# First batch of an mLSTM + Fourier-mix kernel: head outputs with tokens on the partitions instead of transposed afterwards

## The chip, the core and the metric

One core of a Trainium2 chip runs the whole program. The metric is device time in microseconds (us) of one execution, given as the median of several executions; lower is better. Engines are named as in the profile: PE is TensorE (PEld its weight loads), DVE is VectorE, ACT is ScalarE, POOL is GpSimd, SP is the engine that issues the transfers.

## The reference, cut to what matters

Two blocks follow each other. The first is an mLSTM cell with B = 4 batches, H = 8 heads, S = 768 tokens and head dimension D = 40:

```python
for t in range(S):
    m_new = np.maximum(f_gate[:, :, t] + m, i_gate[:, :, t])
    f_stab = np.exp(f_gate[:, :, t] + m - m_new)
    i_stab = np.exp(i_gate[:, :, t] - m_new)
    ...
    C = f_stab * C + i_stab * outer(vt, kt)
    n = f_stab * n + i_stab * kt
    h_tilde = C @ qt
    denom = np.maximum(np.abs(n . qt), 1.0)
    y[:, :, t] = sigmoid(o_gate) * h_tilde / denom
```

Its output, heads side by side, is x with 4 x 768 x 320 numbers. The second block takes the real part of a Fourier transform of x over tokens and over features, adds it to x (u), normalises each row of u, and computes u + relu(un @ w_ch1) @ w_ch2 with a hidden width of 1280. All in float32.

## The kernel before

The recurrence is worked in chunks of L = 128 tokens, NT = 6 chunks for a batch. In a chunk, the output of each head is the sum of two products: one with the state carried in from the chunks before (C and n side by side, 41 columns a head, since the values have a column of ones attached), and one inside the chunk (scores of queries and keys, weighted by a matrix W of exponentials, times the values). Then each head's 40 columns are divided by its 41st and multiplied by the output gate.

The edits are in the first batch (b = 0), whose chunks run by `plan_mlstm`. The order of all work is written by hand: `at(slot, phase, function, ...)` files a step under a time slot and a phase, and `run` issues the steps in that order. Each engine works off its own instructions strictly in the order of issue, so a step filed earlier goes ahead on its engine's queue. For chunk c the slots start at s = 3c. The steps that matter, with their lines:

- `mlstm_scores` (L609): scores ps, 8 heads, with tiles of 64 x 64 of the array.
- `mlstm_exp` (L563): ACT makes W from the PSUM bank pM that PE filled (`spread_max`, L235).
- `mlstm_scale_q` (L571): the queries times their decay, qg. For c = 1 and 2 from PSUM by DVE (L576), later by POOL (L580) after a one-element copy (L579) that reads the finished gate of chunk c-2, so POOL waits for it.
- `mlstm_scale_v` (L582), `mlstm_decay` (L602): POOL prepares values and state.
- `mlstm_weigh` (L618): DVE multiplies scores into W (L622).
- `mlstm_from_state` (L624) and `mlstm_from_chunk` (L633): the two products, added up in the PSUM tile hb (`first_heads_ps`). The state and the values are the weights (64 columns: the 41 of one head, then the first of the next), and the 128 tokens move. So hb holds features on the partitions and tokens along the columns, two heads in a column block.
- `mlstm_to_state` (L639), `mlstm_add` (L658): the next state, pc on PE and the addition on DVE (L661, L663).
- `mlstm_heads` (L647): ACT copies hb, 128 x 512, to SBUF (hT, L650). `mlstm_turn` (L652): PE transposes it in four blocks into the PSUM bank px (L656).
- `mlstm_finish` (L767): DVE takes the 41st columns (den: L785, L786, L787), makes gate over denominator (so, L789), and multiplies (x, L776). The gate's tanh is ACT's (`mlstm_tanh`, L665).
- `mlstm_rows` (L797): in chunks 1 and 4 one row of x has its place in another chunk; three small copies move it (L801 ACT, L803 DVE, L805 ACT).

All products go through `product` (L598), so the profile lists them at L599; the tile names tell them apart. A float32 product shows as two matmul records.

After the chunks come the folds of x for the Fourier transform (`mix_fold`, L895, DVE and POOL), its products (`mix_products`, L975; `mix_feat`, L995), u with its statistics (`mix_add`, L1018), transposes to put (L1065), and the first hidden products (L1163). Pieces of the weights w_ch1, which arrive as 64-bit floats, are put together by DVE in between (`Piece`, L477 to L499). Some products without use (`idle_products`, L143, tile pi) stand on PE ahead of the fold products: each of two products of 256 columns is issued in pieces of 85 or 86 columns, and every piece loads the same 128 x 128 weights. The other three batches use `plan_halves`, which already holds tokens on the partitions and is not touched.

Of the kernel before, what the change touches and what calls it, by code (L numbers as in the profile page):

```python
# [10 lines left out]
FP = mybir.dt.float32  # L11
# [7 lines left out]
B, H, S, D = 4, 8, 768, 40  # L19
L = 128  # L20
NT = S // L
NP = H // 2
LH = L // 2
NS = S // LH
D1 = D + 1
# [5 lines left out]
TG = NT // 2  # L31
# [8 lines left out]
NK = HALF + 2  # L40
# [17 lines left out]
def kernel(  # L58
# [15 lines left out]
    nc = tc.nc  # L74
# [19 lines left out]
    def bank(name, shape, n=None):  # L94

        return ps_m.tile(shape, FP, name=name, tag=f"pm{next(turn) if n is None else n}")


    ident = const.tile([L, L], FP, name="ident")
# [20 lines left out]
    hT_bufs = []  # L120
# [7 lines left out]
    def at(slot, phase, fn, *args):  # L128
        plan.setdefault((slot, phase), []).append((fn, args))
# [10 lines left out]
    def columns_of(n, parts):  # L140
        return [slice(i * n // parts, (i + 1) * n // parts) for i in range(parts)]
# [8 lines left out]
    def gates(gp):  # L150
# [7 lines left out]
        shift = gp.tile([BH, NT, L], FP, name="shift")  # L158
        m_in = gp.tile([BH, NT, 1], FP, name="m_in")
        F = gp.tile([BH, NT, L], FP, name="F")  # L160
        hT_bufs.extend(gp.tile([L, 4, L], FP, name=f"h{n}") for n in range(2))
        M, Mq = (gp.tile([L, NT, L], FP, name=name) for name in ("M", "Mq"))
        g, wk = (x_bufs[1].rearrange("p c m -> p (c m)")[0:n, i * S:(i + 1) * S].rearrange("p (c t) -> p c t", t=L)
                 for i, n in enumerate((L, BH)))
# [355 lines left out]
    chunks = {}  # L520
# [77 lines left out]
    def product(out, w, x, start):  # L598
        nc.tensor.matmul(out, w, x, start=start, stop=True, skip_group_check=True)  # L599
# [24 lines left out]
    def mlstm_from_state(b, c):  # L624

        k = chunks[b, c]
        k.ph = first_heads_ps[:, :, 0:2 * L].rearrange("p hip (m t) -> p hip m t", t=L)
        for p in range(0, NP, 2) if c > 0 else ():
            for hip, i in TILES:
                r, n = slice(hip * 64, hip * 64 + D), (p + i) * D1  # L630
                product(k.ph[half(i), hip, p // 2, :], k.C[0][r, n:n + LH], k.qg[r, p + i, :], p == 0)

    def mlstm_from_chunk(b, c):  # L633
        k = chunks[b, c]
        for h in range(H):
            hip, p = h // NP, h % NP
            product(k.ph[half(p % 2), hip, p // 2, :], k.v[:, h * D1:h * D1 + LH], k.W[:, h, :], c == 0 and p < 2)

    def mlstm_to_state(b, c):  # L639
        k = chunks[b, c]  # L640
# [6 lines left out]
    def mlstm_heads(b, c):  # L647
        k = chunks[b, c]
        k.hT = hT_bufs[c % 2]
        nc.scalar.copy(out=k.hT.rearrange("p (hip m) t -> p hip m t", hip=2), in_=k.ph)  # L650

    def mlstm_turn(b, c):  # L652
        k = chunks[b, c]
        k.px = bank("px", [L, 4, L], 1)
        for n in range(4):
            nc.tensor.transpose(k.px[:, n, :], k.hT[:, n, :], ident)  # L656

    def mlstm_add(b, c):  # L658
        k = chunks[b, c]
# [20 lines left out]
    def half(n):  # L680
        return slice(n * LH, (n + 1) * LH)
# [85 lines left out]
    def mlstm_finish(b, c, part=None):  # L767

        k = chunks[b, c] if part in (0, -1) else chunks.pop((b, c))
        if c == 0:  # L770
            xs[b] = x_bufs[b % 2]
            nc.gpsimd.memset(xs[b][:, :, DM:DM + 1], 0.0)
        h1 = k.px.rearrange("p (a n) (i e) -> p a (n i) e", a=2, i=2) if b == 0 else k.ph
        def tokens(rows, to):
            x, sc = (t.rearrange("p (a h d) -> p a h d", a=2, d=D) for t in (xs[b][rows, to, 0:DM], k.so[rows]))
            nc.vector.tensor_tensor(out=x, in0=h1[rows, :, :, 0:D], in1=sc, op=OP.mult)  # L776

        if part == 1:
            return tokens(slice(0, L), c)
        den = tp.tile([L, H], FP, name="den", tag="den")  # L780

        def two(t):
            return t.rearrange("p (a h) -> p a h", a=2)

        nc.vector.tensor_scalar(out=two(den), in0=h1[:, :, :, D], scalar1=-2.0, scalar2=2.0, op0=OP.mult, op1=OP.max)  # L785
        nc.vector.scalar_tensor_tensor(out=two(den), in0=h1[:, :, :, D], scalar=2.0, in1=two(den), op0=OP.mult, op1=OP.max)  # L786
        nc.vector.reciprocal(out=den, in_=den)  # L787
        sc = k.so.rearrange("p (h d) -> p h d", d=D)
        nc.vector.scalar_tensor_tensor(out=sc, in0=sc, scalar=1.0, in1=den.unsqueeze(2).to_broadcast([L, H, D]),  # L789
                                       op0=OP.add, op1=OP.mult)  # L790
        if b == 0:
            scaled[c] = k.so
        if part != -1:
            tokens(*((slice(0, 1), c - 1) if part == 0 else (slice(0, L), c)))


    def mlstm_rows(b, c, part):  # L797

        spare, x = s_last[0:1, 0:DM], xs[b][0:1, :, 0:DM]
        if part == 0:  # L800
            nc.scalar.copy(out=spare, in_=x[:, c - 1])  # L801
        elif part == 1:
            nc.vector.tensor_copy(out=x[:, c - 1], in_=x[:, c])  # L803
        else:
            nc.scalar.copy(out=x[:, c], in_=spare)  # L805

    def plan_mlstm(b):
        for c in range(NT):
            s, end = 3 * c, c == NT - 1
            if c > 0:  # L810
                at(s, FILL, mlstm_exp, b, c, 0)
                at(s + 1, FILL - 0.5, mlstm_exp, b, c, NP)
                at(s, FILL_PE + (3.5 if end else 2), mlstm_scores, b, c)
            at(s, FILL, mlstm_scale_v, b, c)
            at(s if c == 2 else s + 1, FILL + 0.1, mlstm_scale_q, b, c)
            at(*((6, FILL + 0.25) if c == 1 else (s + 2, FILL)), mlstm_decay, b, c)
            at(s + 1, FILL + (0.2 if end else -0.4), mlstm_weigh, b, c)
            at(s + 2 if end else s + 3, FILL_PE, mlstm_from_state, b, c)
            at(s + 2 if end else s + 3, FILL_PE + (2 if end else 3), mlstm_from_chunk, b, c)
            if not end:  # L820
                at(s + 3, FILL_PE + 3, mlstm_to_state, b, c)
                at(s + 4, FILL - 0.3, mlstm_add, b, c)
            at(*((17, FILL_PE + 2.6) if end else (s + 4, FILL - 0.27)), mlstm_heads, b, c)
            at(*((16, FILL + 0.02) if end else (s + 4, FILL - 0.25)), mlstm_tanh, b, c)
            t, phase = ((5, 2.5), (8, 2.5), (11, 2.5), (14, 2.5), (16, 0.5), (17, 2.8))[c]
            at(t, FILL_PE + phase, mlstm_turn, b, c)
            t, phase = ((6, 0.3), (9, -0.3), (12, -0.3), (15, -0.3), (16.5, 0.4), (18.5, 0))[c]
            if c == 4:
                at(t, FILL + phase, mlstm_finish, b, c, 0)
                at(17, FILL + 0.09, mlstm_finish, b, c, 1)  # L830
            else:
                at(t, FILL + phase, mlstm_finish, b, c)
        for c, part, t, phase in ((1, 0, 7, 0.3), (1, 1, 9, -0.2), (1, 2, 10, -0.1), (4, 0, 16, 0.01),
                                  (4, 2, 18, 0)):
            at(t, FILL + phase, mlstm_rows, b, c, part)

# [138 lines left out]
    def mix_products(p, out, i, m):  # L975
        fm = slice(i * PAD + m.start, i * PAD + m.stop)
        kw = dict(stop=(p == 0), skip_group_check=True)
        if i == 0 and p == TG - 2:
            nc.tensor.matmul(out[:, 0:NK:2], fe[:, p, fm], ds_sb[:, p, 0, 0:NK:2], start=False, **kw)
            nc.tensor.matmul(out[:, 1:NK:2], fe_odd[:, m], ds_sb[:, p, 0, 1:NK:2], start=False, **kw)  # L980
        else:
            nc.tensor.matmul(out, fe[:, p, fm], ds_sb[:, p, i], start=(p == TG - 1), **kw)

    def mix_seq_out(b, i):
        k = mixes[b]
# [9 lines left out]
    def mix_feat(b, p, part=slice(None)):  # L995

        k = mixes[b]  # L1000
        m = slice(COL[p], COL[p] + L)
        if part.start in (None, 0):
            k.pu[p] = bank("pu", [L, DM + 1 + NC], MIX[b - 1]["u"][p] if b > 0 else None)
        pu = k.pu[p]
        if b == 0:
            products = ((pu[:, 0:DM + 1], k.Z[:, 0, m], dd_sb[:, 0]), (pu[:, 0:DM + 1], k.Z[:, 1, m], dd_sb[:, 1]),
                        (pu[:, 0:DM + 1], k.Zt[:, m], dd_sb[:, 2]))
        else:
            products = ((pu[:, 0:NC], k.Z[:, 0, m], dd_sb[:, 0, 0:NC]), (pu[:, NC:DM], k.Z[:, 1, m], dd_sb[:, 1, 1:HALF_D]),
                        (pu[:, 0:DM], k.Zt[:, m], dd_sb[:, 3, 0:DM]))  # L1010
        if p == TG - 2:
            own = first_heads_ps[:, 1, 0:NC] if b == 0 else pu[:, DM + 1:]
            z, zt = (t[:, LAST:LAST + 1].to_broadcast([L, L]) for t in (k.Z[:, 0], k.Zt))
            products += ((own, z, dd_sb[:, 0, 0:NC]), (own, zt, dd_sb[:, 3, 0:NC]))
        for i, (o, z, t) in list(enumerate(products))[part]:
            nc.tensor.matmul(o, z, t, start=(i == 0 or b == 0 and i == 3), stop=(i in (2, 4)), skip_group_check=True)  # L1016

    def mix_add(b, c):  # L1018

# [662 lines left out]
```

## Time and profile before

| What | us |
|---|---|
| median of 3 runs | 379.64 |
| lowest and highest of them | 377.9, 385.28 |
| the profiled execution | 378.71 |
| its span, first to last instruction | 376.9 |

| Engine | busy, us | share of the span |
|---|---|---|
| PE | 370.8 | 98% |
| PEld | 275.6 | 73% |
| DVE | 283.0 | 75% |
| ACT | 171.5 | 46% |
| POOL | 133.2 | 35% |

The granted TensorE clock is 1.0 throughout. A timeline line reads: start, length, engine, source line, operation, tile written <- tiles read, the tile of the array as rows*columns for PE, the size of what moves, and the count of instructions merged into the line. Brackets hold the idle time of that engine before it and what ended that. The end of a matmul is modelled, so spacing is read from start to start. The batch-0 chunks take from about 11 to 40 us of the span, the fold products and feature products from 40 to 55.5.

### The profile page before, as it was taken

To read this page: it belongs to the slowest core of one execution; us is meant where nothing else is said; L and a number is where in the kernel's file an instruction comes from. 1 tells how busy PE (TensorE), PEld (TensorE's weight loads), DVE (VectorE), ACT (ScalarE), POOL (GpSimd) and SP (SyncE) were. 2 spreads that over 40 slices of the span, in tenths; PEclk is the share of its full clock that TensorE was granted. 3 is DMA by queue.
4 is the path that set the end of the run, shared out by engine and by line. 5 is a ranking of instruction groups with operands and counts; after the bars stand their busy time and mean duration, and the time that the engine had idled before them with its cause. 6 is when DMAs were issued, how large, how long until landed. Compare 5 with 4: busy or idle time off the path is not lost.

```text
span 376.9 us, 11439 instructions
## 1 busy us (share of the span) xinstructions
PE 370.8 (98%) x4602; PEld 275.6 (73%) x4602; DVE 283.0 (75%) x668; ACT 171.5 (46%) x502; POOL 133.2 (35%) x241
## 2 busy tenths in 40 slices
PE   8999999999999999999999999999999999999996
PEld 6788555666677777666588999665589996446996
DVE  8898999999998596887955787977745883446552
ACT  5978667657432224754552154845520233445000
POOL 6775424866695114561602434651300000020000
PEclk9999999999999999999999999999999999999999
DMA  7978467999861528550003647300000000000011
GB/s 203 299 227 325 125 194 183 248 260 256 253 188 37 135 77 232 141 143 26 0 3 98 172 123 184 93 3 3 0 2 35 18 19 35 2 0 2 35 37 35
DMA packets 20500, 41.93 MB, mean 111 GB/s; under 512 B 3256, under 2 KB 9744, under 8 KB 20320
## 3 DMA queue, kind: packets, MB, share of 16 engines
q1 hardware_dynamic: 20448, 41.21, 37.7%
q8 instruction: 36, 0.59, 0.7%
q14 instruction: 16, 0.13, 0.1%
HBM read 37.10 MB, written 4.10 MB: 109 GB/s over the span
## 4 chain that ended last, share of the span: by engine, by line
PE 80%; DVE 13%; ACT 2%; issue 2%; DMA 1%; POOL 1%; DVEq 0%; SPq 0%; ACTq 0%; POOLq 0%
PE po L1370 22%; PE pm L1233 17%; PE po L1313 9%; PE pm L1146 6%; PE ph L599 5%; PE pm L1163 4%; PE ps L599 4%; PE pu L1016 3%; PE spare L1233 3%; PE pz L970 2%; PE put L1065 2%; PE pzt L970 1%; DVE e L492 1%; DVE e L477 1%; DVE stats L1039 1%
## 5 line engine op out<-in xcount | busy, mean ns | idle before, releaser
L1319 DVE SCALAR_TENSOR_TENSOR x<-po,rstd,x 128x160 f32<-128x160 f32 (+1 forms) x69 | 27.1, 393 | 35.9 <-PE po L1370 33.2
L595 POOL TENSOR_SCALAR_AFFINE_SELECT W<-W 64x512 f32<-64x512 f32 x36 | 28.1, 780 | 38.5 <-ACT W L568 37.4
L1236 DVE TENSOR_TENSOR h<-h,pm 128x384 f32<-128x384 f32 x52 | 26.7, 549 | 17.6 <-PE pm L1146 8.2
L568 ACT ACTIVATE W<-W,colT 128x64 f32<-128x64 f32 x144 | 36.6, 336 | 0.9 <-DMA W<-M_d 0.9
L722 POOL TENSOR_TENSOR C<-C,decB 128x164 f32<-128x164 f32 x33 | 18.1, 549 | 49.4 <-DVE C L729 45.9
L1313 PE MATMUL po<-w_sb,h 128*128 128x320 f32 x120 | 33.6, 432 | 0.0
L1233 PE MATMUL pm<-uT,w_sb 128*128 128x384 f32 x78 | 31.7, 501 | 0.0
L1089 POOL TENSOR_TENSOR t<-rstd 128x6 f32<-128x6 f32 x12 | 3.7, 311 | 73.0 <-DVE v L1083 72.4
L580 POOL TENSOR_TENSOR qg<-qk,Gb 128x512 f32<-128x512 f32 x21 | 27.2, 1293 | 6.2 <-DMA qk<-in_qkT 5.8
L1146 PE MATMUL pm<-uT,w_sb 64*64 64x384 f32 x288 | 29.3, 496 | 0.0
L1313 PEld LDWEIGHTS po<-w_sb,h 128*128 128x128 f32 x120 | 22.5, 190 | 8.9
L1163 PE MATMUL pm<-uT,w_sb 128*128 128x384 f32 x80 | 28.4, 496 | 0.0
L1370 PE MATMUL po<-T,S 128*128 128x160 f32 x180 | 27.7, 301 | 0.2 <-DVE x L1319 0.2
L1370 PE MATMUL po<-w_sb,h 128*128 128x160 f32 x180 | 26.3, 300 | 0.0
L1370 PEld LDWEIGHTS po<-w_sb,h 128*128 128x128 f32 x180 | 25.2, 190 | 1.4 <-DVE x L1319 0.3
L1370 PEld LDWEIGHTS po<-T,S 128*128 128x128 f32 x180 | 25.4, 190 | 1.1 <-DVE x L1319 0.4
L1296 ACT ACTIVATE h<-h 128x384 f32<-128x384 f32 x45 | 22.5, 520 | 2.5 <-DVE h L1236 2.5
L1163 PEld LDWEIGHTS pm<-uT,w_sb 128*128 128x128 f32 x80 | 14.3, 190 | 10.1 <-issue 1.2
L586 POOL TENSOR_TENSOR vw<-kvt,colT 128x328 f32<-128x328 f32 x23 | 19.3, 840 | 3.9 <-ACT colT L300 2.9
L1233 PEld LDWEIGHTS pm<-uT,w_sb 128*128 128x128 f32 x78 | 13.7, 189 | 8.9 <-DVE h L1236 1.4
L599 PE MATMUL ps<-qk 40*64 40x64 f32 (+1 forms) x768 | 19.6, 235 | 0.5 <-DVE C L729 0.3
L1146 PEld LDWEIGHTS pm<-uT,w_sb 64*64 64x64 f32 x288 | 9.9, 132 | 13.9 <-issue 12.3
(274 smaller groups left out, 839.5 us busy)
## 6 DMA issues: line engine op xcount, KB each, us to landing
kvt<-in_kv SPq DMA_DIRECT2D x24, 336.0 KB
qk<-in_qkT SPq DMA_DIRECT2D x48, 160.0 KB
raw<-in_w SPq DMA_DIRECT2D x10, 640.0 KB
W<-M_d SPq DMA_DIRECT2D x36, 128.0 KB
so<-in_o SPq DMA_DIRECT2D x24, 160.0 KB
out<-x SPq DMA_DIRECT2D x23, 160.0 KB
Gb<-G_d SPq DMA_DIRECT2D x42, 80.0 KB
ds_sb<-in_dft_s SPq DMA_DIRECT2D x1, 1158.0 KB
```

The source lines that it names most:

```text
L568: nc.scalar.activation(out=k.W[:, h, :], in_=M, func=AF.Exp, scale=-1.0, bias=colT[:, c, 0, b * H + h:b * H + h + 1])
L580: nc.gpsimd.tensor_tensor(out=k.qg[:, :, t], in0=k.qk[:, 0, :, t], in1=k.Gb[:, :, t], op=OP.mult)
L595: nc.gpsimd.affine_select(out=W, in_=W, compare_op=OP.is_ge, fill=0.0, base=base, pattern=[[0, H], [-1 if back else 1, LH]], channel_multi ...
L599: nc.tensor.matmul(out, w, x, start=start, stop=True, skip_group_check=True)
L1146: nc.tensor.matmul(banks[i][half(cols)], w1_rest(n)[half(i), half(cols)], u[half(i)], start=start, stop=not start, skip_group_check=True)
L1163: nc.tensor.matmul(k.pm[i], w1_block(ch, f // 2 * 2 + i), u[2 * ch], start=(ch == 0 and not ahead), stop=(ch == 1 and (ahead or n in (2, 5 ...
L1233: nc.tensor.matmul(bank, w, u, start=start, stop=True, skip_group_check=True)
L1236: nc.vector.tensor_tensor(out=h, in0=h, in1=bank, op=OP.add)
L1296: nc.scalar.activation(out=h, in_=h, func=AF.Relu, scale=-1.0)
L1313: nc.tensor.matmul(k.po[m], hidden(gr, f)[:, i * L:(i + 1) * L], w2_sb[:, f, :], start=(f == 0), stop=(f == NFF - 1))
L1319: nc.vector.scalar_tensor_tensor(out=u, in0=po, scalar=k.rstd[:, c:c + 1], in1=u, op0=OP.mult, op1=OP.add)
L1370: nc.tensor.matmul(po, a[:, f], w[:, f], start=start and f == 0, stop=f == half - 1, skip_group_check=True)
```

## The change

The two products swap their sides: W (128 x 128) and the decayed queries qg (40 x 128) are now the weights, and the values and the state, 41 columns a head, move. So hb holds tokens on the partitions and the features along the columns, `mlstm_turn` and the bank px go, and the finishing reads the copy hT, now 128 x 328, from SBUF.

```diff
-        hT_bufs.extend(gp.tile([L, 4, L], FP, name=f"h{n}") for n in range(2))
+        hT_bufs.extend(gp.tile([L, 2, NP, D1], FP, name=f"h{n}") for n in range(2))
...
-        k.ph = first_heads_ps[:, :, 0:2 * L].rearrange("p hip (m t) -> p hip m t", t=L)
-        for p in range(0, NP, 2) if c > 0 else ():
-            for hip, i in TILES:
-                r, n = slice(hip * 64, hip * 64 + D), (p + i) * D1
-                product(k.ph[half(i), hip, p // 2, :], k.C[0][r, n:n + LH], k.qg[r, p + i, :], p == 0)
+        k.ph = first_heads_ps[:, :, 0:NP * D1].rearrange("p hip (m d) -> p hip m d", d=D1)
+        for p in range(NP) if c > 0 else ():
+            for hip in range(2):
+                r = slice(hip * 64, hip * 64 + D)
+                product(k.ph[:, hip, p, :], k.qg[r, p, :], k.C[0][r, p * D1:(p + 1) * D1], p == 0)
...
         for h in range(H):
-            hip, p = h // NP, h % NP
-            product(k.ph[half(p % 2), hip, p // 2, :], k.v[:, h * D1:h * D1 + LH], k.W[:, h, :], c == 0 and p < 2)
+            product(k.ph[:, h // NP, h % NP, :], k.W[:, h, :], k.v[:, h * D1:(h + 1) * D1], c == 0 and h % NP == 0)
...
-        nc.scalar.copy(out=k.hT.rearrange("p (hip m) t -> p hip m t", hip=2), in_=k.ph)
-
-    def mlstm_turn(b, c):
-        k = chunks[b, c]
-        k.px = bank("px", [L, 4, L], 1)
-        for n in range(4):
-            nc.tensor.transpose(k.px[:, n, :], k.hT[:, n, :], ident)
+        nc.scalar.copy(out=k.hT, in_=k.ph)
...
-        h1 = k.px.rearrange("p (a n) (i e) -> p a (n i) e", a=2, i=2) if b == 0 else k.ph
+        h1 = k.hT if b == 0 else k.ph
```

One of the three row copies goes from DVE to ACT, and its slots change; the queries of c = 1 are scaled earlier; the finishing of chunks 0 to 3 stands in slot s + 4, two slots sooner for c = 1 to 3; in chunks 1 and 3 the tanh stands ahead of the copy of hb:

```diff
-            nc.vector.tensor_copy(out=x[:, c - 1], in_=x[:, c])
+            nc.scalar.copy(out=x[:, c - 1], in_=x[:, c])
...
-            at(s if c == 2 else s + 1, FILL + 0.1, mlstm_scale_q, b, c)
+            at(*((2, FILL + 0.55) if c == 1 else (s if c == 2 else s + 1, FILL + 0.1)), mlstm_scale_q, b, c)
...
-            at(*((16, FILL + 0.02) if end else (s + 4, FILL - 0.25)), mlstm_tanh, b, c)
-            t, phase = ((5, 2.5), (8, 2.5), (11, 2.5), (14, 2.5), (16, 0.5), (17, 2.8))[c]
-            at(t, FILL_PE + phase, mlstm_turn, b, c)
-            t, phase = ((6, 0.3), (9, -0.3), (12, -0.3), (15, -0.3), (16.5, 0.4), (18.5, 0))[c]
+            at(*((16, FILL + 0.02) if end else (s + 4, FILL - (0.28 if c in (1, 3) else 0.25))), mlstm_tanh, b, c)
+            t, phase = (s + 4, -0.2 if c > 0 else 0.55) if c < 4 else ((16.5, 0.4), (18.5, 0))[c - 4]
...
-        for c, part, t, phase in ((1, 0, 7, 0.3), (1, 1, 9, -0.2), (1, 2, 10, -0.1), (4, 0, 16, 0.01),
+        for c, part, t, phase in ((1, 0, 7, 0.3), (1, 1, 10, -0.1), (1, 2, 10, -0.09), (4, 0, 16, 0.01),
```

Some products of the first batch's Fourier part are issued in two halves of their columns, each half a matmul with its own weight load:

```diff
-            nc.tensor.matmul(out, fe[:, p, fm], ds_sb[:, p, i], start=(p == TG - 1), **kw)
+            for cols in columns_of(NK, 2):
+                nc.tensor.matmul(out[:, cols], fe[:, p, fm], ds_sb[:, p, i, cols], start=(p == TG - 1 and cols.start == 0), **kw)
...
-            nc.tensor.matmul(o, z, t, start=(i == 0 or b == 0 and i == 3), stop=(i in (2, 4)), skip_group_check=True)
+            for cols in columns_of(o.shape[1], 2 if b == 0 and p == 0 else 1):
+                nc.tensor.matmul(o[:, cols], z, t[:, cols], start=(cols.start == 0 and (i == 0 or b == 0 and i == 3)),
+                                 stop=(i in (2, 4)), skip_group_check=True)
```

## The prediction

> **What bounds the kernel now.** I read the page first (span, share of each engine, chain), then the timeline of PE over the first batch, then the DVE timeline beside it, then single weight loads.
>
> ```profile
> span 376.9 us, 11439 instructions
> PE 370.8 (98%) x4602; PEld 275.6 (73%) x4602; DVE 283.0 (75%) x668; ACT 171.5 (46%) x502; POOL 133.2 (35%) x241
> PE 80%; DVE 13%; ACT 2%; issue 2%; DMA 1%; POOL 1%; DVEq 0%; SPq 0%; ACTq 0%; POOLq 0%
> ```
>
> PE is busy 98% and makes 80% of the chain. DVE's 13% lie nearly all before 75 us. The question is what the first batch (11 to 55 us), where the edits are, does to the moment from which PE runs without a gap. One chunk of it (c = 2, then the start of c = 3) in the PE timeline:
>
> ```profile
> 22.23 0.60 PE L656 MATMUL px<-ident,h 128*128 128x128 f32 x4
> 22.77 0.67 PE L599 MATMUL hb<-qg,C 40*64 40x128 f32 x16
> 23.25 1.05 PE L599 MATMUL ps<-qk 40*64 40x128 f32 x32
> 24.24 1.10 PE L599 MATMUL hb<-W,kvt 128*64 128x128 f32 x16
> 25.16 0.62 PE L599 MATMUL pc<-vw,kvt 128*64 128x41 f32 x16
> 25.71 0.39 PE L232 MATMUL pM<-later_r,ident_b 128*128 128x512 bf16 x1
> ...
> 26.61 0.61 PE L656 MATMUL px<-ident,h 128*128 128x128 f32 x4
> 27.50 0.34 PE L599 MATMUL hb<-qg,C 40*64 40x128 f32 x4 [0.29 <-POOL keep L375]
> ```
>
> Read the starts, not the modelled ends. Every f32 product is two passes, hence x16 for 8. From 22.77 to 27.15 each group starts where the last one's passes run out: one chunk is 4.38 us of PE work. 128 columns at the rate of the 160-column passes at the end of the trace (10 in 1.36 us) (below) are 0.109 us a pass; so px is 4 x 0.11 = 0.44, and the other 0.10 of its 0.54 falls where the tile of the array changes to 40*64.
>
> ```profile
> 358.46 1.52 PE L1370 MATMUL po<-w_sb,S 128*128 128x160 f32 x10
> 359.82 1.52 PE L1370 MATMUL po<-T,S 128*128 128x160 f32 x10
> ```
>
> The one wait in the chunk is at 27.15 to 27.50. DVE shows why, and where it in turn waits for PE:
>
> ```profile
> 24.70 1.23 DVE L803 COPY x<-x 1x320 f32<-1x320 f32 x1
> 25.86 1.27 DVE L622 TENSOR_TENSOR W<-ps,W 128x512 f32<-128x512 f32 x2
> 27.05 0.30 DVE L663 TENSOR_TENSOR C<-C,pc 128x164 f32<-128x164 f32 x1
> ...
> 35.17 1.29 DVE L622 TENSOR_TENSOR W<-ps,W 128x512 f32<-128x512 f32 x2 [0.71 <-PE ps L599]
> ```
>
> The row copy held up the state addition that PE needed at 27.50. At 35.17 DVE idles 0.71 us for the scores of c = 5; from there DVE has no gap until 44.9 (finishing, then the folds), and PE, from 55.54, starts group upon group to the end. So PE sets the time up to 35.17, DVE from there to about 55, PE again after. Whatever the PE work before 35.17 gains or loses is passed on.
>
> **The change, part by part.** Both head products swap sides: the wide operand becomes the weights, only 41 columns move. A pass of 41 columns streams in 41/160 x 0.136 = 0.035 us, so the load of 128 weight columns decides. The nearest row is the filler at 38.22, f32, 128 weight columns, only 85 columns moving:
>
> ```profile
> 38.22 1.42 PEld L147 LDWEIGHTS pi<-rest 128*128 128x128 f32 x12 [0.22 <-issue]
> 39.62 0.60 PE L656 MATMUL px<-ident,h 128*128 128x128 f32 x4
> ```
>
> Twelve loads of 0.19 us (the mean in the groups of f32 128x128 loads) span 1.42: a pitch of (1.42 - 0.19)/11 = 0.112. Streaming 85 columns takes only 0.072, so loading sets it. I take 0.111.
> - Own chunk (from_chunk): now 16 passes in 24.24 to 25.16 = 0.92, two 64-column tiles side by side. New: one tile, 16 x 0.111 = 1.78: +0.85. Bounds: pitch 0.060 (the 32-column transposes at 37.32, six in 0.40, also 128 weight columns, but one-pass) and 0.146 (load plus stream, not overlapped).
> - From state: now 0.48 (four tiles). New: 40 rows x 128 columns, two row tiles. That they load side by side is not in the trace; the 64-row tiles of before do. 8 pairs x 0.111 = 0.89: +0.41. Bounds: 0.48, and 1.78 if they don't pair.
> - Tile changes: the order pM, state, scores, own chunk, pc has two more than before (state to scores, own chunk to pc): +0.20 a chunk, between 0 and 0.40.
> - Transposes: -0.44 each; the 0.10 after them stays, as pM is 128*128 too. Its four queued instructions go from PE, and the bank px with them.
>
> [...]
>
> Sum up to the scores of c = 5: c = 0: 0.85 + 0.10; c = 1 to 4: 4 x (0.41 + 0.85 + 0.20) = 5.84; four transposes (c = 0 to 3) -1.76. Together +5.03.
>
> Waits that go: the row copy moves to ScalarE, where its like (L801, L805) take 0.44 against 1.23 here beside POOL's L580: -0.35 at 27.15 (0 to -0.35). The queries of c = 1 (L576, 0.68) move ahead of L477, L479, L622 and L661; their bank pG is then free before the second pG group, which started at 16.42 though its forerunner ended about 16.12: -0.30 (0 to -0.30). Behind that L576 stands W of c = 1, done 0.7 later, at about 16, and first used at 19.86. **Sum: 5.03 - 0.65 = +4.4.**
>
> Taken at nothing, with the cover:
> - Finishing (den three times, L789, L776; 1.7 us) two slots sooner. Its first instruction now waits in DVE's queue for the head copy L650 of the same slot; behind it stand W and C of the next chunk. W is made 2.8 us before its use (20.14 to 21.4, used at 24.24) and PE will be slower, so nothing is late; without that cover a chunk loses what the copy is late, at most 1.1 (34.50 against the end of its products at 33.40).
> - h is read from SBUF, not PSUM. L776 is 0.49 from PSUM; L904, both operands in SBUF, is 0.47 to 0.79, the latter beside POOL. Before 35 us DVE has the room; c = 4 and c = 5 may lose 0 to 0.6 on the path, kept in the range.
> - The head copy, 512 to 328 columns: 0.59 to about 0.47 (L667, 320 columns). ScalarE is not last. Its tanh ahead of it in c = 1 and 3 delays it 0.4; the three row copies add 0.44.
> - POOL's L579 waits for the finished gate of two chunks before (0.6, 0.5, 0.5 now); that comes sooner, so L580 does. SP's loads of so for c = 4 and 5 wait for the same; they go out sooner, and the rest of SP's queue with them. What this can return: L479 took 1.49 at 48.70 beside POOL's L580, 0.49 at 44.86 without. -1.0 to 0; I take 0.
> - c = 5: own chunk +0.95, transposes -0.44, so the first fold products come 0.5 late on PE; PE later sits idle before put (0.45 at 52.11), which swallows it. Price without that: +0.5.
> - Products cut in two (L982, L1016): 193 columns stream in 0.17 (43.01 to 43.35, two passes), above the 0.111 load, so two halves are the 0.35 of a whole. Bound: 26 more loads x 0.06 = 1.6.
>
> The profiled execution took 378.71 (its span 376.9 and 1.8 around it), which is 0.9 under the median 379.64. Their middle is 379.1, from which I count: +4.4 makes 383.5 (383.1 on the profiled execution, 384.0 on the median).
>
> **The rivals.**
> 1. Not slower: the loads run at the 0.060 pitch of the 32-column transposes. Own chunk 0.96, state 0.48: the sum is 0.14 + 4 x 0.24 - 1.76 - 0.65 = -1.3, so 377.8. It decides below a pitch of about 0.072. For: six such loads in 0.40 us at 37.32. Against: they are one-pass transposes, whose loads last 0.136 to 0.142 where two-pass f32 ones last 0.190; the filler is two-pass, as the new products are.
> 2. Loads not hidden behind the running pass in a full-height tile: pitch 0.146, own chunk 2.34, state 1.17. Sum 1.52 + 4 x (1.42 + 0.69 + 0.20) - 1.76 - 0.65 = +8.3: 387.4. Against: the filler would then need 0.18 a pass. [...] Two row tiles that don't pair (+0.89 a chunk, four chunks) end at the same place, 387.1.
> 3. The delay is partly given back: PE slower leaves DMA and POOL ahead, and DVE, last from 35 to 55, loses its slow L479 (-1.0) and the two L908 of 0.76 against 0.33 beside POOL (-0.9): 381.6. For: DVE's length there is set by such meetings. Against: POOL's own fold L911 causes those of L908, and it moves with DVE.
>
> **How the numbers follow.** The forecast 0.71 (its own range 381.0 to 386.0), rival 1 0.10, rival 2 0.08, rival 3 0.11. The range reaches from below rival 3 to just under rival 2, 380.0 to 387.0, and leaves rival 1 and the top out. A measurement of this kernel can tell about 2%, 7.6 us, from no change. Faster by that needs more than all transposes cost (6 x 0.54): 0.02. Slower by that needs rival 2 or a state product that doesn't pair: 0.09. Within: 0.89.
>
> **What would show it.** The groups hb<-W and hb<-qg turn into 128x41 and 40x41 moving, with starts 1.8 and 0.9 us to the next group, and weight loads 0.11 apart (rival 1: 0.06, rival 2: 0.146); px is gone; a chunk lasts 5.4 us, not 4.4; DVE's wait for the scores of c = 5 ends near 39.6, not 35.17; the first L1163 starts near 59.9, not 55.54, and the span is near 381.3. L803's copy stands on ACT at 0.44. If the first L1163 comes before 56, the step with the load pitch is wrong, or DVE's stretch has shrunk.

## The result and the profile after

| What | before | after |
|---|---|---|
| median, us | 381.21 (6 runs) | 407.31 (6 runs) |
| lowest, highest | 377.9, 385.28 | 402.49, 409.67 |
| profiled execution, span | 378.71, 376.9 | 407.86, 406.2 |
| mean granted clock of it | 1.000 | 0.933 |

The ratio is 1.0666 with a 95% interval of 1.0569 to 1.0763: the change makes the kernel slower by 6.7%. The ratio is taken over the fast executions alone, so it is not quite the quotient of the two medians. The forecast was 383.5, with a range that ended at 387.0. Lines below the edit have moved up: L1163 of before is L1157 after.

The head of the page after, its clock row and its chain; the last line is the clock row of before:

```profile
span 406.2 us, 11437 instructions
PE 400.1 (99%) x4604; PEld 305.2 (75%) x4604; DVE 283.4 (70%) x667; ACT 172.2 (42%) x503; POOL 133.2 (33%) x241
PEclk9765555999999999999999999999999999999999
PE 89%; DVE 8%; issue 1%; DMA 1%; ACT 0%; SPq 0%; DVEq 0%; ACTq 0%
PEclk9999999999999999999999999999999999999999
```

PE's busy time grew by 29.3 us (370.8 to 400.1), exactly as much as the span, with only two matmul records more. So there are no more records; they are longer. The clock row says why: each digit is a slice of 10.2 us, and from the second to the seventh the granted clock is below full speed. Before, all 40 digits are 9. In slices of 0.25 us the clock has only two values: 1.0 to about 14.5, 0.5 to 21.3, 1.0 to 24.7, 0.5 to 72.5, then 1.0 to the end of the work. One chunk inside the long stretch, and the first hidden product, in PE's timeline after:

```profile
39.68 1.94 PE L599 MATMUL hb<-C,qg 40*128 40x41 f32 x16
41.54 1.98 PE L599 MATMUL ps<-qk 40*64 40x128 f32 x32
43.45 3.63 PE L599 MATMUL hb<-kvt,W 128*128 128x41 f32 x16
47.02 1.08 PE L599 MATMUL pc<-vw,kvt 128*64 128x41 f32 x16
...
49.85 1.93 PE L599 MATMUL hb<-C,qg 40*128 40x41 f32 x16
...
85.18 2.20 PE L1157 MATMUL pm<-uT,w_sb 128*128 128x384 f32 x6
```

Read the starts again. A chunk is 10.17 us, not 4.38. Scores (ps), which nobody touched, take 1.91 where they took 0.99. L1157 starts 29.64 later than L1163 did (55.54), which covers the whole difference of the spans, 29.3: behind it nothing more is lost. The stretches of the same trace (columns: length, busy time and count of PE, PEld, DVE, ACT and POOL, granted clock, DMA share, GB/s):

```profile
39.68:49.85 10.17, 10.17 (x91) 8.86 (x91) 4.53 (x10) 4.50 (x18) 3.38 (x5) 0.50 0.47 162
69.00:72.50 3.50, 3.50 (x16) 2.36 (x14) 2.90 (x8) 1.12 (x3) 0.00 (x0) 0.50 0.02 5
72.50:80.00 7.50, 7.50 (x54) 6.08 (x53) 3.46 (x6) 2.89 (x8) 0.18 (x1) 1.00 0.61 170
```

PE is busy for all of the chunk and is still granted half the clock. The clock comes back at 72.5, after 3.4 us in which PE ran fold products of 193 columns.

### The profile page after: what moved, and what is told of

The parts are those of the page before. It is cut to its first block, busy times and chain, and to the rows that moved or that the text cites. A ratio compares the mean times of both kernels' runs of the same rounds, so it can differ in the third digit from the quotient of the medians.

```text
span 406.2 us, 11437 instructions
## 1 busy us (share of the span) xinstructions
PE 400.1 (99%) x4604; PEld 305.2 (75%) x4604; DVE 283.4 (70%) x667; ACT 172.2 (42%) x503; POOL 133.2 (33%) x241
## 4 chain that ended last, share of the span: by engine, by line
PE 89%; DVE 8%; issue 1%; DMA 1%; ACT 0%; SPq 0%; DVEq 0%; ACTq 0%
PE po L1364 20%; PE pm L1227 15%; PE po L1307 8%; PE hb L599 7%; PE pm L1140 6%; PE ps L599 5%; PE ph L599 5%; PE pm L1157 4%; PE pu L1009 3%; PE spare L1227 2%; PE pz L961 2%; PE put L1059 2%; PE pz L974 1%; PE pc L599 1%; PE pzt L961 1%; PE pM L243 1%
## 5 line engine op out<-in xcount | busy, mean ns | idle before, releaser
L568 ACT ACTIVATE W<-W,colT 128x64 f32<-128x64 f32 x144 | 36.6, 336 | 0.1
L1140 PE MATMUL pm<-uT,w_sb 64*64 64x384 f32 x288 | 29.3, 496 | 0.0
L1157 PE MATMUL pm<-uT,w_sb 128*128 128x384 f32 x80 | 28.4, 496 | 0.0
L1083 POOL TENSOR_TENSOR t<-rstd 128x6 f32<-128x6 f32 x12 | 3.7, 312 | 73.0 <-DVE v L1077 72.5
L599 PE MATMUL ps<-qk 40*64 40x64 f32 (+1 forms) x768 | 22.4, 255 | 0.5 <-DVE C L722 0.3
L1157 PEld LDWEIGHTS pm<-uT,w_sb 128*128 128x128 f32 x80 | 14.3, 190 | 10.1 <-issue 1.2
L599 PE MATMUL hb<-kvt,W 128*128 128x41 f32 x96 | 20.5, 399 | 0.0
L599 PEld LDWEIGHTS hb<-kvt,W 128*128 128x128 f32 x96 | 19.6, 311 | 1.2 <-issue 1.0
```

The costliest lines, as they stand in the source:

```text
L568: nc.scalar.activation(out=k.W[:, h, :], in_=M, func=AF.Exp, scale=-1.0, bias=colT[:, c, 0, b * H + h:b * H + h + 1])
L1140: nc.tensor.matmul(banks[i][half(cols)], w1_rest(n)[half(i), half(cols)], u[half(i)], start=start, stop=not start, skip_group_check=True)
L1157: nc.tensor.matmul(k.pm[i], w1_block(ch, f // 2 * 2 + i), u[2 * ch], start=(ch == 0 and not ahead), stop=(ch == 1 and (ahead or n in (2, 5 ...
```

## The experiments

**Theories.** G: a product that moves 41 columns behind a load of 128 weight columns keeps the array streaming for an estimated third of its time (0.035 of 0.111 us), and that lowers the granted clock. Then more columns moved behind the same loads bring the clock back. L: the loads themselves, 128 columns in place of 64, cost the time; then the same loads cost the same however many columns move. F: the finishing, moved sooner and reading SBUF, holds PE up. The kernel before, run alongside on the same chip, took 378.55 us beside runs 1 to 4, 378.89 beside 5 to 8, 379.08 beside 9 to 12 and 379.32 beside 13 to 15 (medians). Runs 1, 4, 5, 12 and 13 were executed several times and are given with a ratio and its interval. The others were executed once, and a single time says little about a few us: the kernel before ran from 377.54 to 387.36 beside them. There the traces have to decide.

**1. Both products wide (e1_both_wide).** The changed kernel; own chunk moves 128 columns, of which 41 are read; the state's 41 columns are moved three times over.

```diff
-  product(k.ph[:, hip, p, :], k.qg[r, p, :], k.C[0][r, p * D1:(p + 1) * D1], p == 0)
+  product(k.ph[:, hip, p, 0:3 * D1]..., k.qg[r, p, :], k.C[0][r, p * D1:(p + 1) * D1].unsqueeze(1).to_broadcast([D, 3, D1]), p == 0)
-  product(k.ph[:, h // NP, h % NP, :], k.W[:, h, :], k.v[:, h * D1:(h + 1) * D1], ...)
+  product(k.ph[:, h // NP, h % NP, 0:L], k.W[:, h, :], k.v[:, h * D1:h * D1 + L], ...)
```

> The changed kernel, but with the moving side of both head products widened from 41 to 128 columns (own chunk: the columns that follow in the same tile) and 123 (state: the 41 columns three times); the extra columns land in unused PSUM and are not read. Weights, loads and the number of products stay. Theory G (gate): the granted clock fell to 0.5 because passes stream 41 columns while 128 weight columns load, so the array is fed a third of the time. Then the clock stays 1.00 over 11 to 75 us, each pass still costs the 0.111 of its load, and the time is what the forecast said at full clock, 381 to 386. Theory L (loads): 128-column loads back to back, or something else of the new order, cause the halving whatever moves. Then the clock is still about 0.5 from 15 to 72 us and the time 402 to 410.

Measured: 385.35, ratio 1.0165 (1.009 to 1.024). The clock is at 0.999 with no half-speed stretch. Its PE timeline:

```profile
19.73 0.43 PE L599 MATMUL ps<-qk 40*64 40x128 f32 x2
20.48 1.10 PE L599 MATMUL ps<-qk 40*64 40x128 f32 x30 [0.33 <-DVE decB L340]
...
25.08 1.16 PE L599 MATMUL hb<-C,qg 40*128 40x123 f32 x16
26.17 1.10 PE L599 MATMUL ps<-qk 40*64 40x128 f32 x32
27.20 2.05 PE L599 MATMUL hb<-kvt,W 128*128 128x128 f32 x16
29.18 0.67 PE L599 MATMUL pc<-vw,kvt 128*64 128x41 f32 x16
...
30.77 1.16 PE L599 MATMUL hb<-C,qg 40*128 40x123 f32 x16
```

Three times the columns, and the chunk falls from 10.17 to 5.69 us. The clock held in all four executions (0.999 to 1.0). G holds and L falls. By the ratios 1.0666 and 1.0165, some 19 of the 25 us lost are the clock (5.0% of 379); in the two profiled executions 22.7 (406.2 against 383.5). What is left, 6.2 us, is the change at full clock, and a little of it is the widening itself: own chunk takes 1.98 and the state 1.09 here, against 1.91 and 1.01 with 41 columns at full clock (e3 and e8, below).

**2. Only own chunk wide (e2_chunk_wide), and 3. only the state wide (e3_state_wide):** one of the two edits of run 1 each.

> Only the own-chunk product is widened to 128 moving columns; the state product still moves 41. Theory G with the own chunk as the cause (1.8 us of every 5.4 at a third): clock 1.00 or nearly, 381 to 387. Theory G with the state product alone being enough (0.9 us at a third per chunk): some windows of half clock, 388 to 400. Theory L: as after, 402 to 410.

> Only the state product is widened (123 moving columns); the own chunk still moves 41. Theory G: the own chunk alone feeds the array too little, so the clock still falls in most of the stretch, 395 to 408. Theory L: 402 to 410. If the state product was the cause, 381 to 387.

Measured: 386.38 for e2, without a half-speed stretch. 392.11 for e3: at half clock from 14.3 to 21.2 and 48.5 to 51.9, at full clock between, so it was milder than G expected (395 to 408). That makes it useful: it shows own chunk with 41 columns at full clock. (A third step at half clock, 96.2 to 99.7, lies far behind the edits, next to a PE wait of 1.52 us.)

```profile
29.55 1.98 PE L599 MATMUL hb<-kvt,W 128*128 128x41 f32 x16
31.46 0.67 PE L599 MATMUL pc<-vw,kvt 128*64 128x41 f32 x16
```

1.91 us from start to start, against 1.78 for the loads and 0.10 for the tile change in the forecast. The load pitch was right, as long as the clock is full.

**8 and 11. Own chunk with 85 columns (e8_chunk_85) and 64 (e11_chunk_64),** state 41: `0:L` and `+ L` of run 1's second edit with 85 and 64.

> The changed kernel with the own chunk moving 85 columns, the state 41: about 66% of a chunk's PE time streams, against 55% in the changed kernel (clock halved), 66% with only the state widened (clock 0.98) and 77% with only the own chunk at 128 (clock 1.00). Theory G with a threshold near 60%: clock 0.97 to 1.00 with a drop in at most one or two windows, 385 to 393. A threshold near 70%: the clock falls for most of the stretch, 395 to 408.

> The changed kernel with the own chunk moving 64 columns (half streamed), the state 41: about 61% of a chunk's PE time streams. With 66% (85 columns) the clock was 0.999, with 55% it was halved from 24.7 to 72.5 us. Theory G: between them; drops in some windows, clock 0.95 to 1.00, 386 to 402.

Measured: 386.99, inside its range, and 406.6, above its range of 386 to 402. The clock rows of the two pages, 85 and then 64 columns:

```profile
PEclk9999999999999999999999999999999999999999
```

```profile
PEclk9955555999999999999999999999999999999999
```

The loads are the same; own chunk takes 1.94 with 85 columns, at full clock, and 3.60 with 64, at half clock (31.09 to 34.69). 21 columns more or less decide 20 us. How much of a chunk streams can be estimated: 0.00085 us a column (0.136/160) times the passes that don't run side by side (8 for the state, 8 for the scores, 16 for own chunk, 8 for pc), with the 0.90 of pM counted in full, over the length of the chunk at full clock. No chunk of the first two kernels of the table ran wholly at full clock, so their 5.55 is itself an estimate. The expectations above used a rougher reckoning, which gave three to five points more.

| Kernel | own chunk, state columns | streams, estimated | clock |
|---|---|---|---|
| changed | 41, 41 | 2.89 of 5.55: 52% | lost, 55 us |
| e11 | 64, 41 | 3.20 of 5.55: 58% | lost, 48 us |
| e3 | 41, 123 | 3.44 of 5.61: 61% | lost at two places |
| e8 | 85, 41 | 3.48 of 5.58: 62% | held |
| e2 | 128, 41 | 4.07 of 5.62: 72% | held |
| e1 | 128, 123 | 4.63 of 5.69: 81% | held |

In this table the order has no exception, but 61 and 62% are one execution each. It is an estimate of means over a chunk, not a threshold of the hardware. It also leaves out waits: e7 (below) streams 2.89 of 4.23 us by the same reckoning, 68%, and lost the clock once where PE stood idle.

**9 and 10. The cost by itself (e9_filler_43, e10_filler_128).** The kernel before, without the change; the filler ahead of the fold products becomes 96 passes with the same loads, of 42 or 43 columns, or of 128.

```diff
-  at(17, FILL_PE + 2.7, idle_products, 2, rest, 3, 3)
+  at(17, FILL_PE + 2.7, idle_products, 8, rest, 3, 6)     # e9
+  at(17, FILL_PE + 2.7, idle_products, 24, rest, 3, 2)    # e10
```

> The kernel before, with its filler ahead of the fold products (12 passes of 85 columns, 1.4 us) replaced by 96 passes of 42 or 43 columns on the same 128x128 weights; nothing of the mLSTM changes. This measures the disputed cost by itself. Theory G: after about one window (3.4 us between the clock's steps in the changed kernel) of a third streamed, the clock falls to 0.50 and the pitch of the passes from 0.111 to 0.222; the filler lasts 14 to 18 us in place of 1.4, and the first fold products run at half clock until a window is full: 393 to 400. If the halving needs something of the mLSTM change, the filler is 96 x 0.111 = 10.7 us at clock 1.00 and the time 386 to 390.

> As the run with 42 or 43 columns, with the same 96 passes and weight loads, but 128 columns moving in each. Theory G: clock 1.00 throughout, the filler 10.6 us, the time 386 to 390. If back-to-back loads of 128 columns lower the clock whatever moves, 0.50 and 393 to 400 here too.

Measured: 396.66 and 390.86. PE's timeline and clock row of e9, then of e10 (a digit is about 9.8 us):

```profile
38.25 16.54 PE L147 MATMUL pi<-rest 128*128 128x42 f32 x96
54.59 1.09 PE L656 MATMUL px<-ident,h 128*128 128x128 f32 x4
PEclk9999659999999999999999999999999999999999
```

```profile
38.01 10.98 PE L147 MATMUL pi<-rest 128*128 128x128 f32 x96
48.83 0.60 PE L656 MATMUL px<-ident,h 128*128 128x128 f32 x4
PEclk9999999999899999999999999999999999999999
```

A third of the columns takes 5.5 us more (starts 16.34 and 10.82 apart). In e9 the clock goes to 0.5 at 42.85 and stays there to 59.92; up to 42.85 the two run alike, 41 passes in the first 4.60 us of either filler. e10 has no half-speed stretch here. With the four transposes px at 1.09 against 0.60 the loss goes on into work that has nothing to do with it. The first hidden product starts at 72.42 in e9 and at 64.10 in e10, 8.3 us apart. The times lie only 5.8 apart, and e10 ends 0.9 above its range, because e10 loses some time far behind the filler: a PE wait of 1.65 us that ends at 101.34 and one step at half clock from 101.46, the 8 in its clock row. So it is shown, apart from every other part of the change, that 42 or 43 columns moving behind the same loads brought the clock to 0.5, and 128 did not. What the clock follows inside the chip is not shown by any trace.

The switches lie on a grid: in the changed kernel 14.46, 21.29, 24.70 and 72.49 are 2, 1 and 14 steps of 3.41 us apart, in e9 42.85 and 59.92 five. The grid does not start with the kernel: the first falls of the changed kernel (14.46), of e11 (21.94) and of e9 (42.85) are not whole steps apart. PE's busy share does not tell which of the two values comes: it is 100% over the chunk at 39.68, at half the clock.

**4, 5, 7 and 13. Column tiles.** Could the transposes go without the wide loads? W and qg are loaded as halves of 64 columns, two tiles side by side, 64 columns moving (e4_narrow_64); the same with the finishing in its old slots (e5_narrow_64_late); with 41 columns moving (e7_narrow_41); and with the finishing reading hb in PSUM, its two halves by turns, in place of a copy (e13_narrow_psum).

```diff
+  for i in range(2):
+      product(k.ph[half(i), h // NP, h % NP, 0:LH], k.W[:, h, half(i)], k.v[:, h * D1:h * D1 + LH], ...)
```

> Tokens on partitions as in the changed kernel, but in column tiles of 64 weight columns, as before: W in two halves of 64 tokens (16 products of 128x64 weights, 64 columns moving), queries in 64x64 tiles, 64 columns moving. Streaming (0.053) and loading (0.053) balance, no transposes. Theory G: clock 1.00; own chunk about 0.93, state about 0.5 as before, a transposing group of 0.44 to 0.54 less per chunk and the two waits gone: 4 x -0.49 - 0.65 = -2.6 before the scores of chunk 5, time 375 to 379 against 379 to 381 of before. A rival that says that the removed transposes or the earlier finishing cause the halving expects half clock and over 390. Theory L gives no halving here.

> The column-tiled form (64 columns moving, no transposes) with the finishing of chunks 0 to 3 and its row copies back in their old slots. In the form with the sooner finishing, decB and the state addition came late behind it on DVE, and PE waited four times (1.04, 0.85, 0.88, 0.95 us) before the folds. Theory F (the sooner finishing costs): with the old slots these waits go, a chunk is 4.0 us of PE against 4.4 of before, and the time is 375 to 378.5. If the waits have another cause (the head copy in SBUF, read by DVE beside POOL), they stay, and the time is 380 to 384.

> The column-tiled form with the sooner finishing, but 41 columns moving per 64 loaded: 0.034 streamed per load of 0.053. Theory G, as a share of streamed time over a window: about 0.8 of a chunk is streamed, so the clock holds as with 64 columns, and the time is 382 to 388 as there. If what counts is the share within the product alone, the clock falls and the time is over 390.

> The column-tiled form, 64 columns moving, sooner finishing, but the head outputs of chunks 0 to 4 stay in PSUM (two halves in turn) and DVE finishes from there; no head copy except in chunk 5. Theory S (reading h from SBUF beside POOL is what costs: den 0.43 in place of 0.16, 0.72 in place of 0.17, x 1.08 and 1.60 in place of 0.49): these return to their PSUM lengths, decB and the state additions come earlier, PE's waits of 0.9 go, and the time is 375 to 379, below before. If PE's own waits without a releaser (about 1 us each, twice as many products) are what costs, they stay, and the time is 380 to 384.

Measured: 386.0 (ratio 1.0194, 1.0091 to 1.0296), 387.63 (1.0249, 1.0193 to 1.0305), 390.33, and 400.53 (1.0565, 1.0525 to 1.0604). None beats the kernel before. e4, e5 and e13 were expected lower; e7's 390.33 with a lost clock is what its expectation gave for the case that the share within the product counts, but a wait stands beside it (below). The clock was not whole in most of these executions either: the profiled one of e4 lost a step at 20.53, and three of the four executions of e4 and of e5 have a mean clock of 0.982 to 0.990, so part of the two medians is the clock. The fastest, 382.75 and 383.65, are the profiled ones. Two prices came out. First, DVE's finishing, from SBUF in e4 and from PSUM in e13 (10 to 45 us; count, busy time, mean ns, idle):

```profile
L771 DVE TENSOR_TENSOR x<-h,so 128x320 f32<-128x320 f32 x6 | 4.6, 772 | 0.2
L780 DVE TENSOR_SCALAR den<-h 128x8 f32<-128x8 f32 x6 | 2.1, 354 | 0.0
L781 DVE SCALAR_TENSOR_TENSOR den<-h,den 128x8 f32<-128x8 f32 x6 | 1.8, 305 | 0.2
```

```profile
L774 DVE TENSOR_TENSOR x<-hb,so 128x320 f32<-128x320 f32 x4 | 2.0, 492 | 0.1
L784 DVE SCALAR_TENSOR_TENSOR den<-hb,den 128x8 f32<-128x8 f32 x4 | 0.7, 166 | 0.1
L783 DVE TENSOR_SCALAR den<-hb 128x8 f32<-128x8 f32 x4 | 0.6, 156 | 0.0
```

From SBUF a finishing costs (772 - 492) + (354 - 156) + (305 - 166) ns = 0.62 us more in the mean (six finishings against four; the step so between them went the other way, 512 ns against 601). Second, e13 pays on PE for leaving out the copy: the state product of a chunk starts only when DVE has finished the chunk right before it, although the two lie in different halves of hb. The wait at 26.73 ends with the x of c = 1 (26.18 to 26.67). So the second half bought nothing; why PE waits for the first is not shown.

```profile
26.73 0.69 PE L599 MATMUL hb<-C,qg 40*64 40x64 f32 x32 [1.98 <-DVE x L774]
...
34.60 1.13 PE L599 MATMUL hb<-C,qg 40*64 40x64 f32 x32 [2.23 <-DVE x L774]
```

With such idle times the clock was lost too, from 20.6 to 24.1 and again, with breaks, from 27.5 to 61.6 (0.957 in the mean). In e7 it was lost from 39.27 to 49.51, beside a wait of 1.89 us that ended at 39.88; with the wait of 0.89 before it, PE stood idle for some 2.2 us of the 3.41 us ahead of 39.27. e5 against e4 shows F to be no cause of what is left: with the old slots the first hidden product starts at 59.26, with the sooner ones at 58.18.

**14. The count of products (e14_before_twice).** e4 and e5 have PE waits that end with no releaser. The kernel before, each head product issued as two of 64 columns with the same weights: more instructions, nothing else.

```diff
-  product(k.ph[half(p % 2), hip, p // 2, :], k.v[:, h * D1:h * D1 + LH], k.W[:, h, :], ...)
+  for i in range(2):
+      product(k.ph[half(p % 2), hip, p // 2, half(i)], k.v[:, h * D1:h * D1 + LH], k.W[:, h, half(i)], ...)
```

> The kernel before with each head product issued as two of 64 moving columns with the same weights: twice the instructions, the same streaming, h and finishing untouched. Theory I (the number of PE instructions makes the waits without a releaser): such waits of about 1 us appear in hb, 380 to 384. Otherwise they do not, and the time is 378 to 380.

Measured: 385.09, one execution, with the same kind of wait. The kernel before ran from 377.63 to 387.36 beside it, so the time decides nothing. PE's timeline of e14, then the waits of e5:

```profile
32.92 0.47 PE L599 MATMUL hb<-qg,C 40*64 40x64 f32 x12
34.87 0.62 PE L599 MATMUL hb<-qg,C 40*64 40x64 f32 x20 [1.48 <-issue]
```

```profile
18.82 0.40 PE L599 MATMUL hb<-C,qg 40*64 40x64 f32 x13 [0.71 <-issue]
...
23.98 0.39 PE L599 MATMUL hb<-C,qg 40*64 40x64 f32 x10 [0.73 <-issue]
...
35.39 0.33 PE L599 MATMUL hb<-C,qg 40*64 40x64 f32 x3 [1.21 <-issue]
```

They fall inside a group, and always at the same places of PE's stream: in e5 after 218, 345, 597, 1104 and 1230 matmul records, in e4 after 218, 724, 1104 and 1230, in e13 after 218, 1104 and 1230, in e14 after 596, 1102 and 1228 (a few records are missing from each trace). The steps are multiples of some 126, and as each matmul has its own weight load (4602 of each on the page of before), of 252 instructions.

Doubled products are not needed for such a wait. e12 (below) has the head products of before, and waits after 1226 and 1352 records, behind the chunks:

```profile
86.39 0.54 PE L599 MATMUL ph<-kvt,W 64*64 64x41 f32 x18 [1.16 <-issue]
...
93.72 0.32 PE L599 MATMUL ps<-vw,kvt 64*40 64x41 f32 x12 [0.77 <-issue]
```

e2, e3, e6, e8, e11 and e15 have one after 1228 records too; the profiled executions of before, of the changed kernel and of e1 have none there. So Theory I, that the number of products makes the waits, is not shown. More products bring more of these places into the chunks; whether PE waits at one differs between kernels with the same products. The page of e14 has a queue for instructions:

```profile
q8 instruction: 37, 0.61, 0.7%
```

37 packets and 0.61 MB make 16.5 KB a packet. With the other instruction queue's 0.13 MB, 0.74 MB for 11,791 instructions is 63 bytes each, so by this estimate a packet holds some 262, near the 252. In e5 a packet of this queue runs 2 to 3 us before each of the three waits ends. So the author's estimate is that PE runs out of instructions where small products use them up faster than they are brought. It is argued from these places and sizes and is not shown: no run changed the queues. Busy queues alone don't explain it: the data queue took 59 to 71% of the transfer engines before the first of the three waits, over 90% before the third, but 24 to 50% before the second. What decides at which place PE waits stays open.

**6, 12 and 15. The small parts.** Run 1 with the finishing and the row copies in their old slots (e6_both_wide_late); the kernel before with only the row copy on ScalarE and the queries of c = 1 sooner (e12_small_edits); run 1 with the Fourier products uncut (e15_both_unsplit).

```diff
-  t, phase = (s + 4, -0.2 if c > 0 else 0.55) if c < 4 else ...                   # e6
+  t, phase = ((6, 0.3), (9, -0.3), (12, -0.3), (15, -0.3), (16.5, 0.4), (18.5, 0))[c]
-  nc.vector.tensor_copy(out=x[:, c - 1], in_=x[:, c])                              # e12
+  nc.scalar.copy(out=x[:, c - 1], in_=x[:, c])
-  for cols in columns_of(NK, 2):                                                   # e15
+  for cols in columns_of(NK, 1):
```

> The changed kernel with both products widened (clock held) and the finishing back in its old slots. Theory F: the 0.7 us wait of the second scores for decB goes, 382 to 385 against 385.1 to 386.0. Otherwise the time stays at 385 to 386.

> The kernel before with only the row copy moved to ScalarE and the queries of chunk 1 scaled earlier. The prediction put these at -0.35 and -0.30 on the path, -0.65 in all: 377.9 to 378.6 where before is 378.9; not more than noise. If DVE's order around them was not on the path, no change.

> The changed kernel with both products widened (clock held), and the Fourier products uncut as before. The prediction put the cut at nothing: 385 to 387.6 as with it. If the added loads cost what they could at most, 1.6 us less.

Measured: 387.63 for e6 and 387.78 for e15, one execution each, both above what was expected and no faster than run 1's 385.35. But their first hidden products start at 62.16 and 62.29, sooner than run 1's 62.51; the rest is waits without a releaser behind 90 us, some 2.2 us in each, which run 1 does not have. In e6 the wait for decB is gone, and PE waits 0.45 us at 30.73 for the row copy instead. e12: 380.26, ratio 1.0008 (0.997 to 1.0046). This interval cannot tell the forecast gain of 0.65 us (0.17%) from nothing; the trace of one execution shows more. The wait at the state of c = 3 is gone, and PE waits as long a step earlier:

```profile
26.54 0.39 PE L243 MATMUL pM<-M,sel 96*128 96x128 bf16 x4
27.32 0.38 PE L232 MATMUL pM<-later_r,ident_b 128*128 128x512 bf16 x1 [0.40 <-ACT W L568]
```

pM's bank is free when ScalarE has made W from it, and the row copy now stands on ScalarE, where it waits 1.38 us for the finished x before it starts at 24.80, with W (L568) behind it. DVE takes up the scores of c = 5 at 36.04, 0.87 later than before (35.17), not 0.65 sooner. e12 is not quite the changed kernel in this: it leaves the row copy in its old slot, and the changed kernel files it a slot later.

## Why the prediction was wrong, point by point

**The step that failed** is the one behind every term: durations of the profile before were carried over to a stretch whose mix of work was new. The 0.111 of the load pitch came from a filler of 12 passes, 1.42 us long. That showed what a pass costs at full clock, and was too short to show what 3.4 us of such passes do to the clock. In the changed kernel the pitch was 3.57/16 = 0.223 at a granted clock of 0.5, and every other group of the stretch took nearly twice its time as well (scores 1.91 for 0.99). The forecast worked out 0.035 us of streaming in 0.111 us of loading and drew from it only that loading sets the time. It had no rival in which the clock changes, and its range ended 20 us short.

**The terms at full clock**, from e1, e2 and e8, where the clock stayed whole through the chunks, and from e3 between 21.15 and 48.46, where it did:

- Own chunk: 1.88 with its tile change forecast, 1.91 measured (e3). Right. In the changed kernel 3.57, for the clock.
- State: 0.99 forecast, with the two row tiles pairing; 1.01 measured (e8). Right.
- Chunk: 5.40 forecast; 5.58 (e8), 5.62 (e2), 5.69 (e1). The 0.2 too little is spread over the borders of the groups: in e8 scores take 1.04 for 0.99 and pc 0.60 for 0.55.
- Transposes: the px groups are gone, as forecast.
- Waits that go, -0.65: in e1 neither is there (the second pG group follows at 17.25, the state of c = 3 at 30.77). The row copy on ScalarE pays only with its new slot: with the old one, e12, W and pM's bank come late behind it.
- Finishing sooner, taken at nothing: wrong cover. The prediction named W and C of the next chunk behind it on DVE. Behind the finishing of c = 0 stand also the second L576 and L340, and the scores of c = 1 wait for L340: in e1 their first two records start at 19.73 and the other 30 at 20.48, some 0.7 later than they would. Undoing the slots (e6) takes this wait away and brings 0.45 at the row copy; the first hidden product comes 0.35 sooner.
- h from SBUF, 0 to 0.6 kept in the range for c = 4 and 5: in e1 the finishing of c = 5 takes 2.22 from start to start, against 1.75 before, 0.47 more; den and x of c = 4 take what they took. Right.
- Products cut in two, at nothing: right as far as one execution tells (e15; the first hidden product 0.2 sooner without the cut).

So at full clock the sum should have been some 6.2 (e1), not 4.4: 0.7 for the scores of c = 1 and 0.2 to 0.3 in each of four chunks make up the difference (0.15 of each chunk is e1's wider products). That alone would have left the time at 385, inside the range; the clock took it out.

**The rivals.** 1 (pitch 0.060) and 2 (0.146) both fall with e3's 1.91, which would have been 1.06 and 2.44 with the tile change. e10 speaks against 2 as well: 96 loads with 128 columns moving behind each take 10.82 us, 0.113 a pass, where load and stream in turn would be about twice that (0.111 and 0.109 by the prediction's estimates). 3 (part given back on DVE) did not come: in e1, DVE takes up the scores of c = 5 at 41.35, 6.18 later than before, and the first hidden product starts at 62.51, 6.97 later. L492 at 52.52 took 1.94 there, against 0.82.

**What would show it**, as announced: px gone and the new shapes there, yes. Groups 1.8 and 0.9 apart, a chunk of 5.4, the first L1163 near 59.9, a span near 381.3: none of these came, first of all because of the clock.

What stays open: what decides on the clock from one grid step to the next, since the estimated shares order the kernels but are means over a chunk, and the first fall of the changed kernel, at 14.46, came only 0.66 us after its first narrow product (13.80), in a grid step that held short waits and small products ahead of it; and what causes the waits without a releaser, late instructions or something else.

## What to carry to other kernels

Before swapping the sides of a product so that few columns move, work out for the stretch around it what share of PE's time streams columns, not what share PE is busy; here, without long waits, the clock held through the chunks at an estimated 62% and above, was lost for short at 61%, and was lost for 48 us and more at 58% and below. When a change slows PE by more than its own terms, read the clock row first, and look at a group that nobody touched: here the scores went from 0.99 to 1.91 us at a granted clock of 0.50. Moving more columns than are needed, 128 (0.109 us by estimate) behind a load of 0.111, cost 0.15 us a chunk here and was worth 19 us.

## What the runs showed of the hardware

- PE at 100% busy was granted half the clock for 47.8 us on end in the changed kernel (24.70 to 72.49); full clock came back only after a grid step filled with products of 193 columns (69.0 to 72.5). Loads slowed down with it: of own chunk's, one lasts 330 ns in the mean from 39.68 to 49.85, at half clock, and 191 from 21.4 to 24.6, at full clock; the 16 passes take 3.57 us there at half clock, 1.91 in e3 at full clock.
- One grid step of 3.41 us of narrow products was enough in e9: its filler began at 38.25, the grid step 39.44 to 42.85 held nothing else, and the clock fell at 42.85. With 128 columns moving (e10) it held.
- The PE waits without a releaser that were counted lie multiples of some 126 matmul records apart and cost 0.2 to 2.0 us each in e5, e12 and e14, also where the products are not doubled (e12).
- The same DVE instruction on 128 x 8 (the first den) takes 0.15 to 0.17 us from PSUM; from SBUF, in e4, 0.16 at 38.22 with POOL idle, and 0.43 at 24.61 beside POOL's L606.
- Order of issue: in the trace of before, the 668 instructions of DVE, the 241 of POOL and 501 of ACT's 502 start in the order in which the program issues them. PE's order is not as strict: its products start in that order but for four places, as at 43.80, where one of L982 starts ahead of one of L979 (44.01) that is issued before it.
